# When to issue three large weight stores: one by one between the steps of the next group's blocks

## The chip, the cores and the metric

The kernel runs on one core of a Trainium2 chip. The metric is the device time of one execution in microseconds (us), lower is better. The engines are TensorE (PE; its weight loads are listed as PEld), VectorE (DVE), ScalarE (ACT), GpSimd (POOL) and SyncE (SP). SP issues every DMA of this kernel on one queue.

## The reference: two layers of linear attention and a gated MLP

The input x has 2048 rows of 512. The same two blocks run twice, with the same weights:

```
x = x + A(layernorm(x))      # linear attention, 32 heads of 16
x = x + B(layernorm(x))      # gated MLP
B(x) = (silu(x @ w1) * (x @ w3)) @ w2     # w1, w3: 512 x 1792, w2: 1792 x 512
```

All arrays are float32.

## The kernel before

**Numbers and blocks.** Every float32 factor is split into a high and a low float16 part, and a product is three float16 products (line 523). In the MLP, a further step replaces 2 x 2 block products by seven products of sums of blocks. So each weight is prepared once: raw float32 blocks are loaded, four sums and differences are formed in place, and high and low parts of the blocks and the sums are written. The inner dimension of 1792 is cut into seven groups of 256. A prepared group of w1 and w3 takes 14 KB in each partition (1792 KB), one of w2 takes 7 KB.

**Sets and passes.** On-chip memory holds four slots for groups of w1/w3. The groups are taken in sets; layer 0 has the sets (0, 1, 2), (3, 4), (5, 6). Each set runs over four passes of 512 rows, c = 0 to 3, and within a pass over its groups. `mlp_group` multiplies with w1 and w3, `first_half` and `second_half` multiply with w2. The MLP of layer 0 runs from about 195 to 600 us, the first set until about 320 us. Layer 1 reads prepared groups back from device memory, so layer 0 stores them there: groups 0 to 4 of w1/w3 are stored in the part that matters here (`w13_d`; line 757), and w2 groups 0 to 2 as well (`w2_d`, same line).

**The background.** During layer 0's MLP a generator, `background`, prepares what later sets need. After each `mlp_group`, `steps(more, budget)` takes pieces from it until their weights use up a budget from the table `HOOKS`. The generator finishes the preparation that attention has left; for groups 0, 1, 2 it prepares w2 (`w2_group`: loads at line 778, splits at lines 412 and 413) and stores it; then it takes w1/w3 group 4 and after it group 3. For group 4 it loads raw blocks (`load_raw`, line 547), stores the prepared groups 0, 1 and 2 from their slots, and makes the blocks (`w13_group`, ten yields: splits at lines 445 and 447, sums at lines 573 to 579). Group 4 is made in the fourth slot and stored from there, since group 3 will take the slot. w2 of group 4 is loaded later (line 778).

**The next rows.** While a pass runs, `mlp_rows` normalises the rows of the next one (line 500), copies them to float16 (line 1277), and transposes the high parts (line 1278) and the low parts (line 1286) by DMA; at its end it stores them (line 1290). It too is taken in pieces after each `mlp_group`.

**Order of the work.** Attention is pinned, instruction by instruction, to the order of the text. The MLP is not: a scheduler orders each engine's and the queue's instructions ahead of time. An instruction's place in the text is its rank, `later(n)` (a priority lowered by n) shifts it, and dependences hold it back. `store` is an exception:

```python
    def store(what, g, src):
        to = {"w13": w13_d, "w2": w2_d}[what]
        with in_order("SP"):
            nc.sync.dma_start(to[:, g], src)
```

`in_order("SP")` puts each such DMA behind the last DMA pinned on SP (in issue, not in completion). At run time each engine and the queue serve their instructions in the order so fixed. ScalarE copies the PSUM banks of the products out (line 1341), applies silu (line 1296), makes the hidden float16 parts (line 1300) and also does the background's splits, all in one queue.

Of the kernel before, what the change touches and what calls it, by code (L numbers as in the profile page):

```python
# [8 lines left out]
F16 = mybir.dt.float16  # L9
# [45 lines left out]
GROUP = 14 * KB  # L55
GROUP2 = 7 * KB
AT_W = 0
# [31 lines left out]
def kernel(  # L89
# [21 lines left out]
    def view(at, dtype, *dims):  # L111
        size = 4 if dtype == F32 else 2
        n = size
        for d in dims:
            n *= d
        ap = arena[:, at // 4 : (at + n) // 4]
        if dtype != F32:
            ap = ap.bitcast(dtype)
        if len(dims) > 1:
            names = "abcdefg"[: len(dims)]  # L120
            ap = ap.rearrange(
                f"p ({' '.join(names)}) -> p {' '.join(names)}",
                **{n: d for n, d in zip(names[1:], dims[1:])},
            )
        return ap
# [151 lines left out]
    @contextmanager  # L277
    def in_order(*engines):

        traced = nc.cur_bb.bb.instructions  # L280
        before = traced[-1]
        depth.append(engines)
        yield
        depth.pop()
        if depth:
            return
        start = next(k for k in reversed(range(len(traced))) if traced[k] is before) + 1
        for i in traced[start:]:
            if str(i.engine).split(".")[-1] not in (engines or PINNED):
                continue  # L290
            if i.engine in pinned:
                tc.add_manual_dep(
                    i,
                    pinned[i.engine].name,
                    mybir.DependencyInfo(
                        mybir.DependencyClass.NoSync, mybir.DependencyReason.DATA
                    ),
                    reason="in_order",
                )
            pinned[i.engine] = i  # L300
# [15 lines left out]
    def scalar():  # L316
        i = next(column)
        return scalars[:, i : i + 1]
# [28 lines left out]
    w13 = {g: view(AT_W + i * GROUP, F16, 2, 2, 2, 7, P) for g, i in SLOT13.items()}  # L347
# [74 lines left out]
    def engine_of(what, i):  # L422
        table = {what: table_of(what, state["layer"])}
        return {"V": nc.vector, "P": nc.gpsimd, "A": nc.scalar}[table[what][i]]
# [14 lines left out]
    def settle():  # L439
        while owed:  # L440
            owed.pop(0)()

    def split_late(hi, lo, src, scale):

        nc.scalar.activation(hi, src, AF.Copy, scale=scale)  # L445
        owed.append(
            lambda: nc.vector.scalar_tensor_tensor(lo, src, scale, hi, OP.mult, OP.subtract)  # L447
        )
# [91 lines left out]
    def load_raw(g):  # L540

        dst = view(AT_RAW, F32, 2, 2, 2, 2, P)
        for w, name in enumerate(("w1", "w3")):
            for c in range(2):
                for h in range(2):
                    at = h * (F // 2) + g * P
                    nc.sync.dma_start(dst[:, w, :, c, h], w_rows[name][:, c, :, at : at + P])

    def w13_group(g, dst):

        if g > 2:
            raw = view(AT_RAW, F32, 2, 2, 4, P)
            quads = [raw[:, :, :, i] for i in range(4)]
            rows = [(w, raw[:, w, :, 2:4], ((0, raw[:, w]),)) for w in range(2)]
        else:
            cols = [slice(h * (F // 2) + g * P, h * (F // 2) + g * P + P) for h in range(2)]
            quads = [st_w13[:, :, c, :, cols[h]] for c in range(2) for h in range(2)]
            both = [
                [
                    st_w13[:, w, c].rearrange("p k (h n) -> p k h n", h=2)[:, :, :, cols[0]]  # L560
                    for c in range(2)
                ]
                for w in range(2)
            ]
            rows = [(w, both[w][1], ((0, both[w][0]), (2, both[w][1]))) for w in range(2)]
        a11, a21, a12, a22 = quads
        scale = [info[n][2] for n in ("w1", "w3")]
        for w, pair, _ in rows:
            split_late(dst[:, w, 0, :, 0], dst[:, w, 1, :, 0], a11[:, w], scale[w])
            yield heavy[0]  # L570
            split_late(dst[:, w, 0, :, 1:3], dst[:, w, 1, :, 1:3], pair, scale[w])
            yield heavy[0]
        engine_of("w13", g).tensor_tensor(a22, a21, a22, OP.add)
        yield 1
        engine_of("w13", g).tensor_tensor(a21, a11, a21, OP.subtract)
        yield 1
        engine_of("w13", g).tensor_tensor(a11, a22, a11, OP.subtract)
        yield 1
        engine_of("w13", g).tensor_tensor(a12, a12, a11, OP.subtract)
        yield 1  # L580
        for w, _, parts in rows:
            for i, src in parts:
                n = src.shape[2]
                to = [dst[:, w, part, :, 3 + i : 3 + i + n] for part in range(2)]
                split_late(to[0], to[1], src, scale[w])
                yield heavy[0] * n / 2
# [167 lines left out]
# [4 lines that stand above are left out]
# [23 lines left out]
    def w2_group(g):  # L781


        raw = w2_raw(g)
        dst, scale = w2_s[g], info["w2"][2]
        yield 1
        split(dst[:, 0, 0], dst[:, 1, 0], raw[:, 0], scale)
        yield 1
        split(dst[:, 0, 1:3], dst[:, 1, 1:3], raw[:, 2:4], scale)
        yield 1  # L790
        later_plain = any(g in gs and plain_run(1, 4 * i + c) for i, gs in enumerate(SETS[1]) for c in range(NC))
        if later_plain or g in w2_a21 and state["plain"]:

            to = w2_a21.get(g, dst[:, :, 6])
            split(to[:, 0], to[:, 1], raw[:, 1], scale)
            if later_plain:
                with in_order("SP"):
                    nc.sync.dma_start(a21_d[:, g], to)
            have.add(("plain", g))
            yield 1  # L800
        a11, a21, a12, a22 = (raw[:, i] for i in range(4))
        for to, a, b, op in (
            (a22, a21, a22, OP.add),
            (a21, a11, a21, OP.subtract),
            (a11, a22, a11, OP.subtract),
            (a12, a12, a11, OP.subtract),
        ):
            engine_of("w2", g).tensor_tensor(to, a, b, op)
        yield 1
        split(dst[:, 0, 3:], dst[:, 1, 3:], raw, scale)  # L810
        yield 2
        have.add(("w2", g))

    def background(first):

        for tasks in first[::-1]:
            yield from tasks.rest()
        a, b, c = SETS[0]
        for g in a:
            yield from w2_group(g)  # L820
            store("w2", g, view(AT_W2 + SLOT2[g] * GROUP2, F16, GROUP2 // 2))
        late = view(AT_W + 3 * GROUP, F16, 2, 2, 2, 7, P)
        for g in b[::-1]:
            load_raw(g)
            if g == b[-1]:
                for i in a:
                    store("w13", i, view(AT_W + i * GROUP, F16, GROUP // 2))
            yield 1
            yield from w13_group(g, late)
            if g == b[-1]:  # L830
                store("w13", g, view(AT_W + 3 * GROUP, F16, GROUP // 2))
            settle()
            have.add(("w13", g))
            while state["plain"]:
                yield 100
            yield from w2_group(g)
        while state["set"] < 1:
            yield 100
        for g in c:
            load_raw(g)  # L840
            yield 1
            yield from w13_group(g, w13[g])
            settle()
            have.add(("w13", g))
            yield from w2_group(g)
# [309 lines left out]
    kept = []  # L1155
# [318 lines left out]

    def mlp(layer, prep):
        more = background(prep) if layer == 0 else iter(())

        def ready_for(what, g):
# [168 lines left out]
    for item in LOADS[0].split():  # L1647
        what, t = item.split(":")
        i = int(what[1:] or 0)
# [21 lines left out]
    with in_order():  # L1671
# [21 lines left out]
        b = scalar()  # L1693
# [56 lines left out]
```

## Time and profile before

| what | value |
|---|---|
| median of 3 runs | 1174.78 us (1173.83 to 1175.29) |
| profiled execution | 1172.7 us |
| its span, first to last instruction | 1170.9 us |
| mean granted TensorE clock | 0.999 |
| PE busy | 1147.1 us, 8862 matmuls |
| DVE, ACT, POOL busy | 832.0, 638.3, 402.8 us |

The profiled execution's time is 1.8 us more than its span: what lies before the first and after the last instruction. A busy share counts an engine's executing instructions; issuing DMAs and waiting don't count. Times of single rows are from the start of the span.

### The profile page before, as it was taken

Reading aid. Unit: us, or ns where it says so; the run is one execution under the profiler, and the core shown is the slowest. Engines: PE = TensorE matmul, PEld = TensorE weight load, DVE = VectorE, ACT = ScalarE, POOL = GpSimd, SP = SyncE. Lnnn points to the kernel's source line nnn. Section 1 sums busy time; section 2 is a strip of 40 time slices with the busy share of each in tenths; the row PEclk is TensorE's granted clock in tenths of the full one; section 3 lists DMA queues with packets and bytes.
Section 4 is the critical chain, followed back from the end, with each engine's and each line's share of the span. In section 5 each row is a group of like instructions: output and inputs, shape, how many; then the busy total and the mean of one; then the engine's idle time right before and its main releaser. Section 6 shows DMA issues by size and latency. Waiting matters only on the chain.

```text
span 1170.9 us, 21807 instructions
## 1 busy us (share of the span) xinstructions
PE 1147.1 (98%) x8862; PEld 863.5 (74%) x8862; DVE 832.0 (71%) x1401; ACT 638.3 (55%) x1078; POOL 402.8 (34%) x472
## 2 busy tenths in 40 slices
PE   8999998999999999999999999998999999999998
PEld 3445444788888888888864454477888888888887
DVE  6798889977977897778674568757856675656533
ACT  6677787856544554444456644766444344443422
POOL 4343588321000222113368715771252110303120
PEclk9999999999999999999999999999999999999999
DMA  9977565979632221112217425654351351111011
GB/s 279 323 235 233 122 172 119 279 257 278 155 129 100 83 81 64 64 64 73 73 41 209 122 84 116 130 144 125 86 140 64 127 189 48 50 67 37 1 37 37
DMA packets 163396, 147.43 MB, mean 126 GB/s; under 512 B 129632, under 2 KB 138976, under 8 KB 158688
## 3 DMA queue, kind: packets, MB, share of 16 engines
q1 hardware_dynamic: 163296, 146.04, 43.2%
q8 instruction: 69, 1.13, 0.4%
q14 instruction: 31, 0.25, 0.1%
HBM read 72.48 MB, written 42.07 MB: 98 GB/s over the span
## 4 chain that ended last, share of the span: by engine, by line
PE 73%; DVE 8%; DMA 6%; ACT 5%; POOL 4%; issue 2%; SPq 1%; POOLq 0%; DVEq 0%; ACTq 0%
PE bb L523 19%; PE po L1388 16%; PE bc L523 10%; PE pk L523 6%; PE gt L523 6%; PE pq L523 5%; PE po L523 5%; PE ba L523 4%; DMA arena<-arena 3%; DMA arena<-in_B_w_dram 3%; PE po L1408 2%; POOL arena L1283 1%; DVE arena L447 1%; DVE arena L1283 1%; DVE arena L1437 1%
## 5 line engine op out<-in xcount | busy, mean ns | idle before, releaser
L523 PEld LDWEIGHTS <-arena 128*128 128x128 f16 x6360 | 618.3, 98 | 251.3 <-issue 11.6
L523 PE MATMUL bb<-arena 128*128 128x256 f16 x2688 | 330.6, 273 | 4.8 <-DMA arena<-arena 2.3
L1388 PE MATMUL po<-arena 128*128 128x256 f16 x1932 | 234.8, 273 | 6.2 <-ACT arena L1300 3.2
L1388 PEld LDWEIGHTS <-arena 128*128 128x128 f16 x1932 | 188.3, 98 | 30.7 <-ACT arena L1300 5.0
L1341 ACT ACTIVATE arena<-bb 128x512 f32<-128x512 f32 x196 | 114.9, 588 | 132.7 <-PE bb L523 99.3
L523 PE MATMUL bc<-arena 128*128 128x256 f16 x1344 | 165.9, 273 | 0.3 <-DVE arena L1344 0.2
L1302 DVE TENSOR_TENSOR arena<-arena 128x512 f16<-128x512 f32 (+1 forms) x90 | 104.4, 1160 | 81.1 <-ACT arena L1300 80.9
L1300 ACT ACTIVATE arena<-arena 128x512 f16<-128x512 f32 x112 | 99.8, 891 | 104.9 <-DVE arena L1297 47.2
L1296 ACT ACTIVATE arena<-arena,scalars 128x512 f32<-128x512 f32 x112 | 74.7, 667 | 120.9 <-DVE arena L1344 119.9
L1297 DVE SCALAR_TENSOR_TENSOR arena<-arena,scalars 128x512 f32<-128x512 f32 x112 | 86.0, 768 | 50.8 <-ACT arena L1296 50.7
L1344 DVE TENSOR_TENSOR arena<-arena,bc 128x512 f32<-128x512 f32 x112 | 76.4, 682 | 57.7 <-ACT arena L1341 42.3
L1302 POOL TENSOR_TENSOR arena<-arena 128x512 f16<-128x512 f32 x22 | 25.5, 1157 | 230.9 <-ACT arena L1300 206.8
L1457 POOL TENSOR_TENSOR arena<-arena 128x512 f32<-128x512 f32 x25 | 35.7, 1428 | 195.7 <-DVE arena L1437 186.1
L1437 DVE SCALAR_TENSOR_TENSOR arena<-po,scalars,arena 128x256 f32<-128x256 f32 (+1 forms) x170 | 91.9, 584 | 6.5 <-PE po L1388 6.2
L523 PE MATMUL po<-arena 128*128 128x512 f16 x384 | 87.8, 379 | 2.1 <-DMA arena<-arena 2.0
L523 PE MATMUL ba<-arena 128*128 128x256 f16 x672 | 88.7, 274 | 0.0
L523 PE MATMUL gt<-arena 128*128 128x512 f16 x384 | 87.6, 379 | 0.6 <-ACT arena L953 0.3
L523 PE MATMUL pk<-arena 128*128 128x512 f16 x384 | 87.7, 379 | 0.0
L523 PE MATMUL pq<-arena 128*128 128x512 f16 x384 | 87.6, 379 | 0.1
L500 ACT ACTIVATE arena<-arena,nb_all,rs_all 128x512 f32<-128x512 f32 x64 | 50.2, 806 | 23.9 <-POOL nb_all L497 21.0
L1408 PE MATMUL po<-arena 128*128 128x256 f16 x480 | 57.0, 273 | 1.8 <-ACT arena L1300 1.8
L447 DVE SCALAR_TENSOR_TENSOR arena<-arena,scalars 128x512 f16<-128x512 f32 (+2 forms) x60 | 50.1, 856 | 7.9 <-ACT arena L445 6.5
(163 smaller groups left out, 1265.2 us busy)
## 6 DMA issues: line engine op xcount, KB each, us to landing
arena<-xb_d SPq DMA_DIRECT2D x12, 1792.0 KB, 6.8
xb_d<-arena SPq DMA_DIRECT2D x8, 1792.0 KB, 6.5
xt_d<-arena SPq DMA_DIRECT2D x32, 256.0 KB, 2.8
arena<-xt_d SPq DMA_DIRECT2D x32, 256.0 KB, 3.0
arena<-in_B_w_dram SPq DMA_DIRECT2D x8, 896.0 KB, 6.5
arena<-in_B_w_dram SPq DMA_DIRECT2D x28, 256.0 KB, 4.1
w_d<-arena SPq DMA_DIRECT2D x4, 1792.0 KB, 10.3
arena<-w_d SPq DMA_DIRECT2D x4, 1792.0 KB, 6.9
```

Source lines behind the costliest of these rows:

```text
L447: lambda: nc.vector.scalar_tensor_tensor(lo, src, scale, hi, OP.mult, OP.subtract)
L500: nc.scalar.activation(dst, x_sb[:, t, :], AF.Identity, scale=rs_all[:, t : t + 1], bias=nb_all[:, t : t + 1],)
L523: nc.tensor.matmul(dst, lhs(a, k), rhs(b, k), start=first and k == 0 and i == 0, stop=last and k == n - 1 and i == len(PASSES) - 1, skip_g ...
L1296: nc.scalar.activation(t, gate, AF.Silu, scale=info["u1"])
L1297: nc.vector.scalar_tensor_tensor(t, up, info["hid"], t, OP.mult, OP.mult)
L1300: nc.scalar.activation(hs[:, 0, lo:hi], t[:, lo:hi], AF.Copy)
L1302: engine.tensor_tensor(hs[:, 1, lo:hi], t[:, lo:hi], hs[:, 0, lo:hi], OP.subtract)
L1341: nc.scalar.activation(dst, bank_, AF.Copy)
L1344: nc.vector.tensor_tensor(dst, dst, bank_, OP.add)
L1388: nc.tensor.matmul(po[:, i * HALF : (i + 1) * HALF], hs[:, a, qx, cs], w2[:, b, qw, :], start=g == ends[0] and i + a + b == 0, stop=g == e ...
L1408: nc.tensor.matmul(acc[n][:, half * HALF : (half + 1) * HALF], hs[:, a, qx, cs], w2_a21[g][:, b] if (i, half) == (0, 1) else w2[:, b, i + ...
L1437: nc.vector.scalar_tensor_tensor(dst, src, cb, to, OP.mult, OP.add)
```

## The change

Before, the three stores of groups 0, 1 and 2 stand in a row in the generator, between group 4's raw load and its blocks. After, the generator's pieces for group 4 are the same with the same weights, and a store is placed in front of the yield of the fourth, the seventh and the tenth of `w13_group`'s ten steps (step numbers 3, 6, 9). Data, sizes, the store of group 4 and the pins are as before.

```diff
         for g in b[::-1]:
             load_raw(g)
             if g == b[-1]:
-                for i in a:
+                pass
+            yield 1
+            kept = list(a) if g == b[-1] else []
+            for step, weight in enumerate(w13_group(g, late)):
+                if kept and step >= (3, 6, 9)[len(a) - len(kept)]:
+                    i = kept.pop(0)
                     store("w13", i, view(AT_W + i * GROUP, F16, GROUP // 2))
-            yield 1
-            yield from w13_group(g, late)
+                yield weight
+            for i in kept:
+                store("w13", i, view(AT_W + i * GROUP, F16, GROUP // 2))
             if g == b[-1]:
                 store("w13", g, view(AT_W + 3 * GROUP, F16, GROUP // 2))
             settle()
```

In the code b is (3, 4), and the loop takes it backwards. The test `g == b[-1]` therefore holds for group 4, the first one taken.

## Rows read from the trace of the kernel before

**Rows 1.** The page's first part: busy us, share of the span, instructions of each engine.

```profile
PE 1147.1 (98%) x8862; PEld 863.5 (74%) x8862; DVE 832.0 (71%) x1401; ACT 638.3 (55%) x1078; POOL 402.8 (34%) x472
```

**Rows 2.** Windows: us, busy of each engine, granted clock, DMA share, GB/s.

```profile
235.00:240.00 5.00, 5.00 (x48) 4.47 (x47) 2.23 (x4) 2.19 (x5) 0.73 (x1) 1.00 0.31 111
...
250.00:330.00 80.00, 78.31 (x713) 69.46 (x711) 64.90 (x103) 45.36 (x74) 8.53 (x10) 1.00 0.77 229
...
250.00:272.00 22.00, 22.00 (x204) 19.71 (x202) 17.59 (x26) 12.15 (x21) 2.88 (x4) 1.00 1.08 339
...
252.50:266.70 14.20, 14.20 (x132) 12.72 (x131) 13.38 (x20) 7.87 (x13) 1.88 (x3) 1.00 1.04 402
...
309.00:313.00 4.00, 2.40 (x23) 2.00 (x22) 2.99 (x6) 2.11 (x4) 0.00 (x0) 1.00 0.51 149
...
330.00:575.00 245.00, 244.77 (x2238) 218.46 (x2236) 194.31 (x330) 113.24 (x181) 55.00 (x50) 1.00 0.25 85
...
575.00:600.00 25.00, 23.66 (x193) 18.52 (x191) 16.76 (x27) 11.19 (x16) 10.05 (x11) 1.00 0.01 1
```

**Rows 3.** Timeline of SP, 150 to 420: start us, us, line, operation, out<-in.

```profile
221.42 1.64 SPq L547 DMA_DIRECT2D arena<-in_B_w_dram  x3
...
224.31 0.88 SPq L757 DMA_DIRECT2D w_d<-arena  x1
...
246.56 1.03 SPq L757 DMA_DIRECT2D w_d<-arena  x1
247.76 3.08 SPq L547 DMA_DIRECT2D arena<-in_B_w_dram  x4
250.89 1.52 SPq L757 DMA_DIRECT2D w_d<-arena  x3
252.51 14.18 SPq L1278 DMA_TRANSPOSE arena<-arena  x1
266.78 3.05 SPq L1286 DMA_TRANSPOSE arena<-arena  x1
269.93 0.53 SPq L757 DMA_DIRECT2D w_d<-arena  x1
270.51 1.79 SPq L778 DMA_DIRECT2D arena<-in_B_w_dram  x2
```

**Rows 4.** Timeline of PE, 175 to 345; idle time before, its end, in brackets.

```profile
194.86 2.29 PE L523 MATMUL bb<-arena 128*128 128x256 f16 x10 [2.29 <-DMA arena<-arena]
...
312.10 1.47 PE L523 MATMUL bb<-arena 128*128 128x256 f16 x12 [1.60 <-ACT arena L1341]
```

**Rows 5.** Timeline of ACT, 215 to 345, with the same brackets.

```profile
236.81 1.52 ACT L412 ACTIVATE arena<-arena,scalars 128x256 f16<-128x256 f32 x3 [2.37 <-DMA arena<-in_B_w_dram]
...
248.86 1.04 ACT L1277 ACTIVATE arena<-arena 128x1024 f16<-128x1024 f32 x1
...
271.10 1.88 ACT L1277 ACTIVATE arena<-arena 128x512 f16<-128x512 f32 x3 [0.82 <-DMA arena<-arena]
...
277.97 1.37 ACT L412 ACTIVATE arena<-arena,scalars 128x256 f16<-128x256 f32 x2 [0.39 <-DMA arena<-in_B_w_dram]
...
309.81 1.76 ACT L412 ACTIVATE arena<-arena,scalars 128x256 f16<-128x256 f32 x3 [1.63 <-DMA arena<-in_B_w_dram]
```

**Rows 6.** The chain that ended last, 195 to 345: start us, us, what.

```profile
270.99 7.61 DMA arena<-in_B_w_dram
...
302.41 2.48 DVE arena L447 x2
...
306.67 4.16 DMA arena<-in_B_w_dram
```

**Rows 7.** Timeline of DVE, 245 to 270.

```profile
264.51 2.48 DVE L447 SCALAR_TENSOR_TENSOR arena<-arena,scalars 128x1024 f16<-128x1024 f32 x2 [0.36 <-ACT arena L445]
```

**Rows 8.** Windows of 2 us behind the wait at 194.86.

```profile
195.00:197.00 2.00, 2.00 (x11) 1.37 (x10) 1.97 (x6) 0.98 (x2) 2.00 (x2) 0.50 0.26 50
197.00:199.00 2.00, 2.00 (x15) 1.56 (x14) 1.06 (x3) 1.97 (x6) 2.00 (x3) 0.71 0.43 123
```

## The prediction

> **What bounds the kernel now.** I began with the page's busy shares [rows 1]: TensorE is busy for 1147.1 of 1170.9 us. All it can ever give back is 23.8 us, and only where a change makes one of its waits shorter. So I went to the stretches around the first set of layer 0's MLP [rows 2]. From 250 to 272 us, when the three stores are moved, PE is busy for 22.00 of 22.00 us. From 250 to 330 it is busy for 78.31 of 80.00: it loses 1.69 us, and 1.60 of them between 309 and 313, where it is busy for 2.40 of 4.00. From 330 to 575 it loses 0.23 of 245 us. What is near the stores can therefore return 1.7 us at most, 0.14% of the time.
>
> Third I read the order on SP's queue [rows 3]. The three stores (line 757) are issued at 250.89, 1.52 us for all three. Right behind them stands the first of two transposes of the next rows (line 1278), which holds the queue for 14.18 us, until 266.7, while the stores drain; the second (line 1286) follows at 266.78. The fourth store is issued at 269.93, the loads for group 4's w2 blocks at 270.51. This is what looks wrong in the profile, and the reader is to see that PE does not feel it: the 22 us of [rows 2] cover the hold from end to end.
>
> Last I asked which wait does reach PE [rows 4, 5]. ScalarE's queue is served in order. At 309.81 splits of w2 (line 412), 1.76 us of them, follow 1.63 us of waiting for a load; the copy of a PSUM bank (line 1341) comes behind them, and PE starts at 312.10 after 1.60 us idle for that copy. The load that belongs to the stores' neighbourhood is that of 270.51: it took 7.61 us to land [rows 6], and ScalarE's split of it waited 0.39 us, at 277.97. So a load that lands later there meets a queue with hardly any slack.
>
> **The change part by part.** *Removed and added:* no instruction, no byte. Seven stores of this kind run before and after, three of them elsewhere in the program's text. Issue is 1.52 us on SP for three, the same for one by one, and SP does no arithmetic. Zero.
>
> *Moved in the text.* The generator gives the same steps with the same weights, so the hooks' budgets take the same pieces; only the stores fall later, past step 3, 6 and 9 of group 4's ten. But the order in the text isn't the order of issue: outside the pinned part the scheduler takes what is ready, and the text only ranks what is ready together. The rows show it. Group 4's raw load is written after all three w2 stores of groups 0 to 2, yet its first half is issued from 221.42 on, before the first of them, at 224.31; its other half, whose buffer was still in use, at 247.76 [rows 3]. The three stores are held by one thing, the pin of `store` behind the last pinned store on SP, at 246.56. Their data is done: the first pass has multiplied with groups 0 to 2. After the change they hang on the same pin, on no step of group 4. So they are ready at the same moment as before, and the next thing on SP that could overtake them is the first transpose, whose last input, a copy on ScalarE of 1.04 us at 248.86 [rows 5], ends at 249.90. Either the three are still issued in a row, and nothing has changed, or one or both transposes get in front of some of them.
>
> *If the transposes get in front.* The 14.18 us of hold go, or shrink to what is left of a store or two. One store's transfer is 1792 KB, 1.835 MB, at the 402 GB/s of the stretch from 252.5 to 266.7 [rows 2]: 4.6 us, so behind one store the transpose is held some 5 us. What does an earlier landing give? ScalarE's next row copies waited 0.82 us for these transposes, to 271.10 [rows 5], and PE waited for nothing then. Bounds: from nothing (PE had no idle time there) to the 0.09 us that PE lost in this stretch outside 309 to 313, plus, if the whole background chain up to the w2 load before 309.81 moves forward with it, the 1.60 us. I take nothing: that load (306.67) follows the last splits of group 3's blocks (line 447, 302.41) in the chain of waits [rows 6], and those wait for no transpose of these rows.
>
> *What is late instead.* Every store that goes behind a transpose drains later, and the queue serves the fourth store and the w2 loads behind it. Before, the three were gone by 266.7, so only the fourth store lay ahead of the loads. In the worst order the third store goes only as step 9 is done (its last splits on VectorE, line 447, end at 264.51 + 2.48 = 266.99 [rows 7]); then its 4.6 us stand in front, the loads land near 283.2 instead of 270.99 + 7.61 = 278.6 [rows 6], and the split waits 0.39 + 4.6 = 5.0 us. What PE pays is bounded by two rows of ScalarE: the wait of 2.37 us before 236.81 cost PE nothing (from 235 to 240 it is busy for 5.00 of 5.00 us [rows 2]); the wait of 1.63 us before 309.81 cost 1.60 [rows 4, 5]. So between nothing and 5.0 us; I take the middle of 5.0 - 2.4 = 2.6, with the cover of the first row, and 5.0, with that of the second: 3.8. This is the price of a rival, not of the forecast, since nothing makes the stores wait for the steps.
>
> *The ranks of others.* The lines between the old and new places move up by three in the text. What runs under a lowered priority there may swap with a neighbour, and the scheduler may then order engines a little differently further on. The nearest rows for what that can move: the 1.69 us lost near the stores and the 1.34 us lost from 575 to 600 [rows 2], where layer 0 ends. Either sign; I take nothing.
>
> *The skill.* The Trainium skill, page "DMA: Bandwidth & Descriptors", section "Queues, rings and completion order", says that each DMA engine consumes a queue's descriptors in ring order. By this rule, spreading the stores saves no transfer time and only chooses what stands behind them; the loads at 270.51 could only get later. The trace agrees: the loads of 256 KB behind the fourth store took 7.61 us [rows 6].
>
> The sum: 0 us. The profiled execution took 1172.7 us, its span of 1170.9 and 1.8 around it, and is 2.1 us below the median of the three runs, 1174.78. The forecast stands on the median: 1174.8. A difference of 0.2%, 2.3 us, is about the least that can be told from no change here, since the three runs lie within 1.5 us.
>
> **The rivals.**
>
> *The queue doesn't change.* The stores stay in a row, as above; the time is the forecast's. I put it inside the forecast, as its likelier half.
>
> *Slower: late loads hold ScalarE.* The third store (or two) drains in front of the w2 loads. It decides from about 2.4 us of extra lateness on. For it: the slack of 0.39 us, and DMA already at 1.08 of 16 engines' time from 250 to 272 [rows 2]. Against it: the stores are ready by 247 and SP is free to issue them. 1174.8 + 3.8 = 1178.6 us. A gap of that length may cost the clock too: PE stood 2.29 us before 194.86, and the granted clock was 0.50 and 0.71 in the next two stretches of 2 us [rows 4, 8], the first of them at the lower of the two levels, 1.2 GHz; that took (0.50 + 0.29) x 2 = 1.6 us, and would make 1180.2. The Trainium skill, page "TensorE: Matmul & The Clock Gate", section "Part 1: The HAM clock gate", says the same, that an idle TensorE falls back to half rate until it has been busy again.
>
> *Faster: the losses near and after the stores vanish.* The chain of rows and w2 blocks runs ahead, ScalarE no longer stands before 309.81, and the end of the layer falls better. All of 1.69 + 1.34 = 3.0 us: 1171.8. For it: the hold of 14.18 us is real and is released. Against it: two places 260 us apart would both have to gain, and either alone stays under 2.3 us.
>
> **How the numbers follow.** The forecast, no change that can be told, has 0.62 (0.37 the same queue, 0.25 transposes in front at no gain to PE); late loads 0.20; losses gone 0.18. Each rival lies beyond 0.2%, so these are also the chances of same, slower and faster. The forecast's own range is 1172.5 to 1177.1. The range for 8 in 10 reaches to the faster case, 1171.8, and nearly to the slower one, 1178.5; beyond them I leave half of the slower case and a little of the faster, under 2 in 10.
>
> **What would show it.** On SP: whether three issues of line 757 still stand in one row before the transpose of line 1278, and whether that one still takes about 14 us. On ScalarE: the wait before the first line 412 of group 4, 0.39 us before; over 2.4 us means the slower rival. On PE: 22.00 of 22.00 us where the stores drain, and 1.60 us at 312. What would make me wrong: PE idle time in a place that has nothing to do with the stores, in the second set or in layer 1, from a schedule that has come out otherwise; no row of before prices that.

## The result, and the profile after

The changed kernel is slower: 1179.91 us median (1179.52 to 1180.88, six runs) against 1175.58 us (1173.83 to 1177.66, six runs) on the same chip. The ratio is 1.0043, 95% interval [1.0032, 1.0053]. That is above the upper end of the predicted range, 1178.5 us.

The profile after is one execution of 1179.52 us, span 1177.6 us. Its line numbers behind the edit are those of before plus 6 (L1278 is L1284, L1341 is L1347, L1388 is L1394). The first part of the page answers to [rows 1]:

```profile
PE 1147.1 (97%) x8862; PEld 863.4 (73%) x8862; DVE 832.7 (71%) x1401; ACT 638.8 (54%) x1078; POOL 402.8 (34%) x472
```

TensorE does the same work in the same 1147.1 us; the span grew by 6.7 us, all of it idle time. The windows of [rows 2] again, in the kernel after:

```profile
250.00:330.00 80.00, 75.96 (x689) 66.99 (x687) 61.24 (x98) 43.13 (x70) 7.24 (x9) 1.00 0.70 217
250.00:272.00 22.00, 20.84 (x192) 18.52 (x190) 18.43 (x28) 13.96 (x23) 6.08 (x8) 1.00 1.06 337
...
309.00:313.00 4.00, 4.00 (x39) 3.60 (x37) 4.00 (x7) 0.72 (x1) 0.00 (x0) 1.00 0.01 4
330.00:575.00 245.00, 242.10 (x2206) 215.31 (x2205) 194.70 (x329) 112.62 (x179) 54.53 (x51) 1.00 0.26 89
575.00:600.00 25.00, 24.27 (x212) 20.46 (x210) 15.90 (x27) 9.66 (x15) 9.79 (x11) 1.00 0.00 1
```

The reader is to see two things. The old gap is gone (309 to 313: 4.00 of 4.00, before 2.40). But 250 to 330 lost 4.04 us instead of 1.69, and 330 to 575 lost 2.90 instead of 0.23. The granted clock stays at 1.00. The first matmul of layer 1 that both traces show behind the same small gap (gt, L523) starts at 613.96 us before and at 619.91 after, 5.95 us later; the other 0.75 us of the 6.7 fall behind it, where every engine's order is the same in both kernels.

What became of SP's queue ([rows 3] before):

```profile
246.51 1.03 SPq L757 DMA_DIRECT2D w_d<-arena  x1
247.71 3.08 SPq L547 DMA_DIRECT2D arena<-in_B_w_dram  x4
250.83 0.47 SPq L757 DMA_DIRECT2D w_d<-arena  x1
251.40 6.41 SPq L1284 DMA_TRANSPOSE arena<-arena  x1
257.90 3.30 SPq L1292 DMA_TRANSPOSE arena<-arena  x1
261.26 1.06 SPq L757 DMA_DIRECT2D w_d<-arena  x2
263.52 0.32 SPq L1296 DMA_DIRECT2D xb_d<-arena  x1
267.55 3.07 SPq L547 DMA_DIRECT2D arena<-in_B_w_dram  x3
270.66 1.57 SPq L757 DMA_DIRECT2D w_d<-arena  x1
272.28 3.85 SPq L778 DMA_DIRECT2D arena<-in_B_w_dram  x2
```

One store, then both transposes, then two stores. The hold shrank from 14.18 to 6.41 us. But more moved than the stores: the store of the transposed rows (L1296, 272.50 us before) and three of group 3's raw loads now go ahead of the fourth store, and the loads of w2 go behind them. (The fourth store is group 4's. The page counts four stores of 1792 KB, those of groups 0, 1, 2 and 4; group 3's prepared weights are not stored.)

TensorE from 250 to 450 us, every line with idle time ahead of it ([rows 4] before, where 312.10 was the only one in this stretch):

```profile
265.03 1.47 PE L523 MATMUL bb<-arena 128*128 128x256 f16 x12 [1.16 <-ACT arena L1347]
...
302.11 1.47 PE L523 MATMUL bb<-arena 128*128 128x256 f16 x12 [1.11 <-ACT arena L1347]
...
322.19 1.47 PE L523 MATMUL bb<-arena 128*128 128x256 f16 x12 [0.99 <-ACT arena L1347]
...
325.23 1.59 PE L1394 MATMUL po<-arena 128*128 128x256 f16 x13 [0.70 <-ACT arena L1306]
...
330.69 1.47 PE L523 MATMUL bc<-arena 128*128 128x256 f16 x12 [0.60 <-DVE arena L1303]
...
367.91 1.59 PE L1394 MATMUL po<-arena 128*128 128x256 f16 x13 [0.49 <-ACT arena L1306]
...
374.26 0.39 PE L1394 MATMUL po<-arena 128*128 128x256 f16 x2 [0.17 <-ACT arena L1306]
...
381.07 1.59 PE L1394 MATMUL po<-arena 128*128 128x256 f16 x13 [0.93 <-ACT arena L1306]
...
431.76 0.49 PE L1394 MATMUL po<-arena 128*128 128x256 f16 x3 [0.30 <-DVE arena L1443]
...
432.48 0.39 PE L1394 MATMUL po<-arena 128*128 128x256 f16 x2 [0.24 <-ACT arena L1306]
```

Ten small waits, 6.69 us together, in place of one of 1.60. None is for a DMA. Each is for a copy out of PSUM (L1347), a finished hidden part (L1306) or a step of VectorE on the same data (L1303, L1443). ScalarE's timeline shows what stood in front of them ([rows 5] before):

```profile
262.10 1.89 ACT L1283 ACTIVATE arena<-arena 128x512 f16<-128x512 f32 x3 [1.62 <-DMA arena<-arena]
263.89 0.61 ACT L1306 ACTIVATE arena<-arena 128x512 f16<-128x512 f32 x1
264.41 0.57 ACT L1347 ACTIVATE arena<-bb 128x512 f32<-128x512 f32 x1
...
284.55 0.51 ACT L412 ACTIVATE arena<-arena,scalars 128x256 f16<-128x256 f32 x1 [0.17 <-DMA arena<-in_B_w_dram]
...
299.00 0.51 ACT L445 ACTIVATE arena<-arena,scalars 128x256 f16<-128x256 f32 x1 [4.57 <-DMA arena<-in_B_w_dram]
299.42 0.71 ACT L1302 ACTIVATE arena<-arena,scalars 128x512 f32<-128x512 f32 x1
300.94 0.63 ACT L1306 ACTIVATE arena<-arena 128x512 f16<-128x512 f32 x1 [0.82 <-DVE arena L1303]
301.48 0.58 ACT L1347 ACTIVATE arena<-bb 128x512 f32<-128x512 f32 x1
...
320.75 0.91 ACT L412 ACTIVATE arena<-arena,scalars 128x256 f16<-128x256 f32 x2 [2.88 <-DMA arena<-in_B_w_dram]
321.56 0.57 ACT L1347 ACTIVATE arena<-bb 128x512 f32<-128x512 f32 x1
```

Row copies (L1283) wait 1.62 us for the transposes ahead of the L1347 for which TensorE waits at 265.03; a split (L445) waits 4.57 us for a load, and the L1347 of 302.11 comes three places behind it; splits of w2 (L412) wait 2.88 us ahead of the L1347 of 322.19. The place that the slower rival named is quiet: the first L412 of group 4 waits 0.17 us, at 284.55. The Trainium skill, page "PSUM — Partial Sum Buffer", section "Engine vs sequencer instructions", says that ScalarE's and VectorE's queues are strictly first in, first out, and that matmuls start in program order; the trace agrees: at 299.00 everything behind the waiting split waited with it.

So the scheduler had made its order anew. Comparing the two built programs, 993 of TensorE's 8845 instructions stand elsewhere, all among its numbers 1495 to 2903, 156 of VectorE's 1369, 92 of ScalarE's 1026 and 28 of SP's 326; none of GpSimd's, and none behind some 435 us.

### The profile page after: what moved, and what is told of

Read it like the earlier page. It is cut to its first block, busy times and chain, and to the rows that moved or that the text cites. A ratio compares the mean times of both kernels' runs of the same rounds, so it can differ in the third digit from the quotient of the medians.

```text
span 1177.6 us, 21810 instructions
## 1 busy us (share of the span) xinstructions
PE 1147.1 (97%) x8862; PEld 863.4 (73%) x8862; DVE 832.7 (71%) x1401; ACT 638.8 (54%) x1078; POOL 402.8 (34%) x472
## 4 chain that ended last, share of the span: by engine, by line
PE 67%; DVE 12%; DMA 7%; ACT 6%; POOL 5%; issue 3%; SPq 1%; DVEq 0%; POOLq 0%; ACTq 0%
PE bb L523 17%; PE po L1394 14%; PE bc L523 9%; PE pk L523 6%; PE gt L523 5%; PE pq L523 5%; PE po L523 5%; DMA arena<-arena 4%; PE ba L523 4%; DMA arena<-in_B_w_dram 3%; PE po L1414 2%; DVE arena L1443 1%; POOL arena L1289 1%; DVE arena L1350 1%; DVE arena L413 1%
## 5 line engine op out<-in xcount | busy, mean ns | idle before, releaser
L523 PEld LDWEIGHTS <-arena 128*128 128x128 f16 x6360 | 618.7, 98 | 254.6 <-issue 14.7
L523 PE MATMUL bb<-arena 128*128 128x256 f16 x2688 | 329.8, 273 | 7.1 <-ACT arena L1347 4.5
L1394 PE MATMUL po<-arena 128*128 128x256 f16 x1932 | 234.4, 273 | 8.6 <-ACT arena L1306 5.3
L1394 PEld LDWEIGHTS <-arena 128*128 128x128 f16 x1932 | 187.9, 98 | 34.5 <-ACT arena L1306 8.4
L1347 ACT ACTIVATE arena<-bb 128x512 f32<-128x512 f32 x196 | 115.0, 589 | 134.1 <-PE bb L523 104.6
L523 PE MATMUL bc<-arena 128*128 128x256 f16 x1344 | 165.9, 273 | 1.2 <-DVE arena L1303 0.6
L1306 ACT ACTIVATE arena<-arena 128x512 f16<-128x512 f32 x112 | 99.8, 891 | 103.2 <-DVE arena L1321 44.3
L1303 DVE SCALAR_TENSOR_TENSOR arena<-arena,scalars 128x512 f32<-128x512 f32 x112 | 86.0, 767 | 51.8 <-ACT arena L1302 51.6
L1443 DVE SCALAR_TENSOR_TENSOR arena<-po,scalars,arena 128x256 f32<-128x256 f32 (+1 forms) x170 | 91.8, 582 | 6.2 <-PE po L1394 5.9
L523 PE MATMUL po<-arena 128*128 128x512 f16 x384 | 87.8, 379 | 2.0 <-DMA arena<-arena 2.0
L523 PE MATMUL ba<-arena 128*128 128x256 f16 x672 | 89.5, 275 | 0.0
L523 PE MATMUL gt<-arena 128*128 128x512 f16 x384 | 87.6, 379 | 0.6 <-ACT arena L959 0.3
L523 PE MATMUL pk<-arena 128*128 128x512 f16 x384 | 87.6, 379 | 0.5 <-DMA arena<-arena 0.3
L523 PE MATMUL pq<-arena 128*128 128x512 f16 x384 | 87.6, 379 | 0.1
L500 ACT ACTIVATE arena<-arena,nb_all,rs_all 128x512 f32<-128x512 f32 x64 | 50.1, 806 | 24.1 <-POOL nb_all L497 21.1
```

Source lines behind the costliest of these rows:

```text
L500: nc.scalar.activation(dst, x_sb[:, t, :], AF.Identity, scale=rs_all[:, t : t + 1], bias=nb_all[:, t : t + 1],)
L523: nc.tensor.matmul(dst, lhs(a, k), rhs(b, k), start=first and k == 0 and i == 0, stop=last and k == n - 1 and i == len(PASSES) - 1, skip_g ...
L1303: nc.vector.scalar_tensor_tensor(t, up, info["hid"], t, OP.mult, OP.mult)
L1306: nc.scalar.activation(hs[:, 0, lo:hi], t[:, lo:hi], AF.Copy)
L1347: nc.scalar.activation(dst, bank_, AF.Copy)
L1394: nc.tensor.matmul(po[:, i * HALF : (i + 1) * HALF], hs[:, a, qx, cs], w2[:, b, qw, :], start=g == ends[0] and i + a + b == 0, stop=g == e ...
```

## The experiments

Most kernels are the kernel before with its text untouched and a table that chains each engine's instructions of this stretch in a given order (no instruction is added, no semaphore either):

```python
for item in table.split():
    at, n = (int(v) for v in (item + "+1").split("+")[:2])
    for i in by[engine][at : at + n]:
        if before is not None:
            tc.add_manual_dep(i, before.name, ...)   # NoSync
        before = i
```

Numbers in the tables are an engine's instructions in the text's order. On SP, 154 to 156 are the three stores, 157 and 158 the two transposes, 160 the fourth store, 162 and 163 the w2 loads of group 4, 159 the store of the transposed rows.

For all of them, this is what TensorE lost from 250 to 450 us in the profiled execution (200 less its busy time there), beside the ratio of the times. The row for the kernel before, from its windows:

```profile
250.00:450.00 200.00, 198.09 (x1804) 175.91 (x1802) 164.76 (x269) 104.62 (x167) 31.30 (x31) 1.00 0.46 147
```

| kernel | lost, us | ratio to before [95%] |
|---|---|---|
| before | 1.91 | 1 |
| after | 6.94 | 1.0043 [1.0032, 1.0053] |
| e1 queue only | 3.03 | 1.0000 [0.9991, 1.0009] |
| e2 copies back | 8.40 | 1.0041 [1.0026, 1.0056] |
| e3 w2 loads first | 6.42 | 1.0026 [1.0014, 1.0037] |
| e4 both back | 5.68 | 1.0030 [1.0018, 1.0041] |
| e5 first part after | 5.27 | 1.0017 [1.0007, 1.0027] |
| e6 second part after | 5.27 | 1.0026 [1.0016, 1.0036] |
| e7 two stores late | 7.64 | 1.0051 [1.0036, 1.0065] |
| e8 after, held | 5.73 | 1.0048 [1.0034, 1.0063] |
| e9 splits behind | 7.41 | 1.0057 [1.0043, 1.0070] |
| e10 one copy ahead | 2.27 | 1.0005 [0.9997, 1.0014] |
| e11 matmul order only | 14.52 | 1.0121 [1.0102, 1.0140] |
| e12 all but matmuls | 16.16 | 1.0134 [1.0114, 1.0154] |
| e13 steps 1, 2, 3 | 3.99 | 1.0002 [0.9990, 1.0013] |
| e14 steps 2, 4, 6 | 8.50 | 1.0053 [1.0037, 1.0069] |
| e15 steps 9, 10, 11 | 11.44 | 1.0084 [1.0067, 1.0101] |
| e16 w2 rows swapped | 6.67 | 1.0048 [1.0033, 1.0063] |

What is lost in this stretch goes with the time, roughly: after minus before is 5.03 us, and 0.0043 of 1175.58 is 5.06. That the two meet so closely is luck, since each row is one execution. Built, e13 is the program of before, instruction by instruction, and its row is 3.99, not 1.91; e8 is the program of after, and its row is 5.73, not 6.94.

The column counts idle time alone. In before, after and e8 the granted clock stayed at 1.00 in this stretch. Behind one gap each in e4, e7, e14 and e15, and behind two in e11, it fell to the lower level, 1.2 GHz: in e7 it was 0.80 from 312 to 316 us and 0.78 from 316 to 320. That is (0.20 + 0.22) x 4 = 1.7 us more, which the column leaves out.

I had two readings to tell apart at first: the order made anew, or the moved transfers themselves.

**e1: the stores moved, nothing else.** Every engine's order is that of before; in the queue alone, the transposes overtake two stores.

```diff
 "SP": 154
-155 156 157 158
+157 158 155 156
 160 162+2 159
```

> The kernel before with one thing moved on SP's queue: the two transposes of the next rows stand behind the first of the three stores and in front of the other two, as in the kernel after. All engines and the rest of the queue are held in the order of before. Theory A (the loss comes from the other instructions that the scheduler has put in another order): the time of before within 0.2%, 1173.5 to 1178 us; the first transpose is held about 6 us instead of 14, and PE loses no more than before from 250 to 330 us, 1.7 us. Theory B (the loss comes from stores that now drain in front of the fourth store and the loads of w2): the loads land up to 4.6 us later, ScalarE's split of them waits up to 5 us instead of 0.39, and the time is 1178 to 1180 us.

1175.38 us, ratio 1.0000. Its queue:

```profile
251.15 0.50 SPq L757 DMA_DIRECT2D w_d<-arena  x1
251.75 7.00 SPq L1278 DMA_TRANSPOSE arena<-arena  x1
258.85 2.81 SPq L1286 DMA_TRANSPOSE arena<-arena  x1
261.71 5.88 SPq L757 DMA_DIRECT2D w_d<-arena  x3
267.63 2.58 SPq L778 DMA_DIRECT2D arena<-in_B_w_dram  x2
```

The hold is 7.00 us instead of 14.18, and nothing is gained or lost. The moved stores are out as the cause; the loads that moved with them are put back in e3.

**e8: the control.** The whole order of after, held by the table over the text of before.

```diff
-"PE", "DVE", "Activation", "SP": order of before
+"PE", "DVE", "Activation", "SP": order of after
```

> Control: the kernel before with every engine and the queue held in the order of the kernel after; the same order as after, instruction by instruction. All theories: the time of after, 1179 to 1181 us; anything else would mean that holding an order costs or saves time by itself.

1180.43 us, ratio 1.0048. The program so built is that of after, instruction by instruction, and its time is that of after: the tables reproduce an order and add nothing of their own.

**e2, e3, e4: which part of the order?** All three hold the order of after, with the row copies (by the lines of before, ScalarE's L1277 and L500, VectorE's L1283) put back where before had them; with the fourth store and group 4's w2 loads put back ahead of the row store; and with both.

```diff
 e2  "Activation": 351 352 353 365 366, "DVE": 459 460 461
+     each behind its neighbour in the order of before
 e3  "SP":
+160 162 163
 159
```

> The kernel after, in its own order, with one thing put back: on ScalarE the three float16 copies of the last rows and two normalisations, and on VectorE the three subtractions behind the copies, stand where they stood before. Theory A1 (the copies that were put in front of the work for PSUM wait for transposes that are not done, and hold ScalarE): the 1.16 us that PE is idle before 265.0 go, with the same loss afterwards; 1178.3 to 1179 us, 0.1% less than after. Theory A2 (the loss is the chain of loads and blocks behind it): the gaps from 302 us on stay and make up at least 3 us of the 5 to 6. If the copies set everything: the time of before.

> The kernel after, in its own order, but on SP's queue the fourth store and group 4's two w2 loads stand in front of the store of the rows and of group 3's raw loads, as before. Theory A2 (the loads of w2 that were put behind these free the second half of the staging buffer late, so group 3's blocks and w2 come late and ScalarE stands waiting for them): group 3's second raw half lands by 293 instead of 299 us, the waits of 4.57 and 2.88 us on ScalarE shrink, the gaps at 302, 322 and 330 us shrink with them, and the time is 1176 to 1177.5 us. Theory A1 (only the copies): no change from after, 1179.5 us.

> Both of the last two together: the copies where they were, and the fourth store and the w2 loads in front. The stores still stand one before and two behind the two transposes. If the two mechanisms make up the loss: 1175 to 1176.5 us, the time of before within 0.2%. If it comes from the order of the matmuls or of ScalarE's and VectorE's other instructions further on, which stays as in after: 1178 us or more.

e2: 1180.37 us. The gap at 265 went, one of 0.63 came at 292.00, and that of 374.26 grew from 0.17 to 1.78 us (at 376.36). The copies aren't the loss. e3: 1177.91 us, but not by what was expected: layer 0 ends where it did (gt at 619.76, after 619.91), with gaps of 1.01, 1.07 and 0.93 us at 265.10, 302.14 and 380.57, where after has 1.16, 1.11 and 0.93. Its 2 us came in layer 1, whose orders are the same (555.74 us from gt to the end, after 557.69). Most of them lie in one wait of TensorE for VectorE (L1437, in after L1443): 0.38 us at 830.44, in after 1.66 us at 832.49. The same wait is 0.42 us in e7, which is no faster than after. I can't say why; one profile of each can't settle it. e4: 1178.16 us, with fewer but larger gaps (2.11 us at 302.88). No single suspect carries it.

**e5, e6: which half?** At some 320 us all engines' orders hold the same instructions behind them, so each can be cut there and joined. By a drain the expectations mean the tail of the last matmul before a gap, which the profile counts as busy: 12 matmuls alone take 1.47 us, 24 in one piece 2.78 (before, 215.25), so a gap adds some 0.16.

```diff
 "PE" 1943, "DVE" 484, "Activation" 382, "SP" 180
+e5: order of after up to these, then that of before
+e6: order of before up to these, then that of after
```

> All engines and the queue have the order of the kernel after up to about 320 us, where the first set ends, and the order of before from there on; the cut lies where both orders have issued the same instructions. Theory F (the first set: w2 and group 3's blocks come late, and whatever stands behind them pays): 1178.5 to 1180 us, with gaps again between 320 and 440 us. Theory S (the second set: the order of ScalarE and TensorE from 320 to 440 us leaves the gaps at 325, 331, 368, 381 and 433 us that were the same in four traces): the gaps up to 302 us stay, 1.16 + 1.11 us less the 1.60 of before, and the time is 1176 to 1177 us.

> The other half: the order of before, with the three stores in a row, up to about 320 us, and the order of after from there on. No store is issued where it was moved to. Theory S: the gaps from 325 to 433 us are there, some 3 us with 0.2 us of drain each, and the time is 1178.5 to 1180 us. Theory F: the time of before within 0.2%.

1177.23 and 1177.83 us, ratios 1.0017 and 1.0026. Neither theory came as priced: both halves lose, and within their intervals they add up to the whole, 0.43%. In e6 the three stores stand in a row as before, and it loses no less than e5.

**e7: two stores much later.** Groups 1 and 2 are stored after group 3's w2 blocks; the order is left to the scheduler.

```diff
-                for i in a:
-                    store("w13", i, view(AT_W + i * GROUP, F16, GROUP // 2))
+                store("w13", a[0], view(AT_W + a[0] * GROUP, F16, GROUP // 2))
...
+            if g == b[0]:
+                for i in a[1:]:
+                    store("w13", i, view(AT_W + i * GROUP, F16, GROUP // 2))
```

> The kernel before, but the stores of groups 1 and 2 stand in the text behind group 3's w2 blocks, where the profile of before has little traffic (from 313 to 330 us DMA is busy for 0.21); group 0's stays. Nothing is held, so the scheduler makes an order of its own: on SP group 3's first raw loads come in front of the fourth store and the w2 loads, as in after, and the transposes stand behind one store. If traffic in front of the loads made the loss: the time of before or up to 1.7 us less. If the order does: a loss like that of after, 1178 to 1181 us, though 3584 KB have left the place.

1180.51 us, ratio 1.0051, with gaps of 1.08, 1.46 and 2.88 us at 265.97, 294.90 and 313.92: another order, other gaps, the same size of loss. Behind the last of them the clock fell as told under the table, so that some 1.7 us of this execution are the clock's.

**e9, e10: who stands in front?** My theory by now: splits that wait for a load stand in front of copies. e9 is the order of after with those steps put behind; e10 is the order of before with its one such place mended.

```diff
 e9  "Activation"            "DVE"
-    351+3 ... 306           478 ... 415
+    306 351+3               415 478
-    380 ... 341             512 514 ... 513 437
+    341 380                 437 512 514 513
-    394 396 358
+    358 394 396
-    446+2 391 399, 488 403 406
+    391 399 446+2, 403 406 488
 e10 "Activation"
-    394 396 395 343
+    343 394 396 395
```

> The order of the changed kernel on all engines, but on ScalarE and VectorE the steps that waited for a load stand behind the copies of PSUM that they held up: ScalarE's copies of the last rows behind the next L1341, one L445 split of 256 columns behind the L1341 that followed it, two L412 splits behind the next L1341, the two L445 splits of 1024 columns and one of 512 behind the next L1341; VectorE's L447 and L413 of the same blocks behind the L1297 and the L1315 after them. Theory (in the re-made order, splits that wait for a load or for VectorE hold up the copies that empty PSUM): the gaps of TensorE at about 265, 302, 322, 325, 368 and 374 us (1.16, 1.11, 0.99, 0.70, 0.49 and 0.17 us, 4.62 us together, and some 0.17 us of drain for each, 1.0 us) go, those of 330.7 (0.60), 381 (0.93) and 432 us (0.54) stay, and the time falls by 4 to 5.6 us: ratio to the kernel before 0.9995 to 1.001. Rival (the new order of the matmuls itself runs out of finished hidden parts, whoever stands in front of whom): the gaps come back some microseconds later, the sum of them up to 450 us stays above 5 us, and the ratio is 1.003 or more.

> The kernel before in its own order on every engine but for one step: ScalarE's copy L1341 that ran at 311.48 us stands ahead of the three L412 splits of 309.81 us, which wait 1.63 us for their load, not behind them. Theory (such a place is what costs the changed kernel its time): the gap of 1.60 us of TensorE at 312.10 us goes with its drain of some 0.17 us, nothing comes later in its place, ratio to the kernel before 0.9983 to 0.9988, some 1173.5 us. Rival (a gap closed there is taken up by the next wait, since the loads are no sooner): the gap moves to between 313 and 335 us with at least half its size, ratio 0.9993 to 1.0005.

Both fell to the rival. e9: 1179.89 us, ratio 1.0057, nothing won. Its TensorE:

```profile
305.39 1.47 PE L523 MATMUL bb<-arena 128*128 128x256 f16 x12 [0.52 <-ACT arena L1341]
...
328.48 1.47 PE L523 MATMUL bc<-arena 128*128 128x256 f16 x12 [1.47 <-DVE arena L1297]
...
369.40 0.83 PE L1388 MATMUL po<-arena 128*128 128x256 f16 x6 [1.46 <-DVE arena L1302]
```

and ScalarE ahead of the first of them:

```profile
304.13 0.72 ACT L445 ACTIVATE arena<-arena,scalars 128x512 f16<-128x512 f32 x1 [2.83 <-DMA arena<-in_B_w_dram]
304.76 0.58 ACT L1341 ACTIVATE arena<-bb 128x512 f32<-128x512 f32 x1
```

The next split of the chain now does what the mended one did. e10: 1174.27 us, ratio 1.0005; the 1.60 us at 312.10 are gone, and 0.81 stand at 313.85. Its other gaps, 0.36 at 275.11, 0.54 at 378.29 and 0.16 at 427.74, can't be put down to the edit. The program of before, executed again in e13, has gaps at the first two places without it:

```profile
275.23 1.47 PE L523 MATMUL bb<-arena 128*128 128x256 f16 x12 [0.48 <-DVE arena L1350]
...
313.48 1.47 PE L523 MATMUL bb<-arena 128*128 128x256 f16 x12 [2.01 <-ACT arena L1347]
...
379.86 1.47 PE L523 MATMUL bb<-arena 128*128 128x256 f16 x12 [1.19 <-ACT arena L1347]
```

So the mended gap did shrink, but the times show no gain: the theory asked for 0.9983 to 0.9988. A waiting step ahead of a copy is how a gap looks, not what the loss hangs on.

**e11, e12: one engine's order against the others'.** e11 takes TensorE's order of after and all else of before; e12 the reverse.

```diff
-e11 "PE": order of before
+e11 "PE": order of after
-e12 "DVE", "Activation", "SP": order of before
+e12 "DVE", "Activation", "SP": order of after
```

> TensorE issues its matmuls in the order of the changed kernel (993 of its 8845 stand elsewhere), while ScalarE, VectorE, GpSimd and the queue of SyncE keep the order of the kernel before, three stores in a row included. Theory P (the matmul order is what is dear: it asks for a finished hidden part or a free buffer of PSUM some hundred ns too soon): gaps of TensorE between 250 and 435 us of 5 us and more together, ratio to the kernel before 1.003 to 1.006. Theory Q (the order on the other engines and of the loads is what is dear): gaps there of under 3 us, as before, ratio 0.9990 to 1.0012. Theory M (each order fits only its own partner): as P in this run, or worse.

> The other half: TensorE keeps the matmul order of the kernel before, while ScalarE, VectorE and the queue of SyncE have that of the changed kernel, with the store, two transposes, two stores, the loads of the second set's group 3 ahead of the fourth store. Theory P: gaps of TensorE between 250 and 435 us of under 3 us together, ratio 0.9990 to 1.0012. Theory Q: 5 us and more, above all where ScalarE's copies wait behind splits (near 265, 302 and 322 us), ratio 1.003 to 1.006. Theory M: as Q in this run, or worse, so that both mixes are slower than the kernel before.

1189.43 and 1190.78 us, ratios 1.0121 and 1.0134: each mix loses some three times what the whole order of after loses. From e12's TensorE:

```profile
346.59 1.47 PE L523 MATMUL bb<-arena 128*128 128x256 f16 x12 [3.20 <-ACT arena L1341]
...
364.50 1.48 PE L523 MATMUL bc<-arena 128*128 128x256 f16 x12 [1.69 <-DVE arena L1297]
```

Theory M held. The loss sits neither in the matmul order of after alone nor in the orders of the others alone: each is dearer with the partner from before than the two are together.

**e13 to e16: is it the stores at all?** Three other placings between the steps, and an edit that touches no store. The order is left to the scheduler.

```diff
-                if kept and step >= (3, 6, 9)[len(a) - len(kept)]:
+                if kept and step >= (1, 2, 3)[len(a) - len(kept)]:    e13
+                if kept and step >= (2, 4, 6)[len(a) - len(kept)]:    e14
+                if kept and step >= (9, 10, 11)[len(a) - len(kept)]:  e15
...
-        for i, f in enumerate((g, NG + g)):                            e16
+        for i, f in ((1, NG + g), (0, g)):
```

> The changed kernel, but its three stores stand behind steps 1, 2 and 3 of group 4's blocks, not 3, 6 and 9; the order is made anew. Theory L (the change costs by the order that happens to be made anew, not by the place of the stores): gaps of TensorE in other places between 250 and 435 us with another sum, so a ratio that is its own, anywhere from 0.998 to 1.007. Theory F (stores between the steps are themselves dear, since they let transposes and loads in between): 1.003 to 1.006, as with the changed kernel, with gaps in the same places (265, 302, 322, 325 us).

> As the run before, with the stores behind steps 2, 4 and 6; its order stands nearer to that of the changed kernel than the other two. Theory L: near the changed kernel where the orders agree, else a ratio of its own between 0.998 and 1.007. Theory F: 1.003 to 1.006.

> As before, with the stores behind steps 9, 10 and 11, which lets both transposes and more of the loads in front of the stores. Theory L: a ratio of its own between 0.998 and 1.007. Theory F: 1.003 to 1.006 or, as more of the transfers come ahead of the stores, above that.

> The kernel before with its stores in a row; only the two loads of each w2 group stand in the other sequence in the text (the second half of the rows first). The same bytes move, no store is touched, and the order is made anew on all engines between 190 and 435 us. Theory L: a ratio of its own, off 1.000 by over 0.002 to either side, with gaps of TensorE in new places. Theory F: 0.999 to 1.001, gaps as in the kernel before.

e13: 1175.09 us, ratio 1.0002. Its stores stand between steps in the text, but not in the program. Built, it is the kernel before, instruction by instruction on every engine and on the queue, with the same waits; so it moved nothing, and is a second measurement of the kernel before. Its queue shows the old row of three and the old hold:

```profile
251.14 1.56 SPq L757 DMA_DIRECT2D w_d<-arena  x3
252.80 14.43 SPq L1284 DMA_TRANSPOSE arena<-arena  x1
```

e14, 1.0053, and e15, 1.0084, were made anew, each with gaps of its own (2.12 us at 382.63 in e14; 1.85 at 261.95 and 2.11 at 386.72 in e15). In e15 the last two stores stand behind the last of the ten steps, and its ratio lies above the range that theory L gave it. And e16, which touches no store and keeps the row of three with its hold, loses as much as the change:

```profile
252.01 1.86 SPq L757 DMA_DIRECT2D w_d<-arena  x3
253.92 14.03 SPq L1278 DMA_TRANSPOSE arena<-arena  x1
```

1180.86 us, ratio 1.0048, with these among its gaps from 250 us on:

```profile
281.04 1.70 PE L1408 MATMUL po<-arena 128*128 128x256 f16 x14 [1.29 <-ACT arena L1300]
...
309.53 0.39 PE L1388 MATMUL po<-arena 128*128 128x256 f16 x2 [2.65 <-ACT arena L1300]
```

Not all of e16's loss lies in this stretch, since its order changes from some 200 us on: at 222.45 TensorE waits 2.59 us (before 1.57 at 220.91), the granted clock is 0.50 from 224 to 226 us, and from 190 to 250 us TensorE gets through 433 matmuls instead of 457, some 2.6 us' worth. From 250 to 450 us it loses 6.67 us, the program of before 1.91 and 3.99.

Stores moved in the queue and every engine's order kept (e1): nothing. Order made anew, in part or whole, and the three stores in a row (e6, e16): 0.26 and 0.48%. That settles what the loss belongs to, the order made anew and not the moved stores. Which part of the order it is, no run shows.

## Why the prediction was wrong

*What bounds the kernel*: right. TensorE is the bound, the hold of SP was covered, and releasing it gave nothing (e1). "What is near the stores can therefore return 1.7 us at most" is right too, as a bound on a gain: the gap of 1.60 us did go. It bounds no loss, and I let it stand for both signs.

*Removed and added: zero*: right, by e1.

*Moved in the text*: right on the stores. Of its two cases the second came, and e13 is the first, at 1.0002. But the two cases leave out that other transfers may change places as well: the row store and three raw loads went ahead of the fourth store.

*If the transposes get in front*: right. The hold fell to 6.41 us, where I had some 5, and PE gained nothing by it.

*What is late instead*, the slower rival: the loads of group 4's w2 were issued 1.77 us later (272.28), but the split that I named waited 0.17 us, not over 2.4, since it had been moved as well (284.55 instead of 277.97). The 1.6 us of clock that I put on top didn't come either: the granted clock stayed at 1.00 behind all ten waits. That rival's time, 1178.6, came near what was measured by another mechanism than its own, which is luck.

*The ranks of others: "either sign; I take nothing"*: this step failed. I priced it at the idle time of the nearest rows, 1.69 and 1.34 us, and set it to nothing. In fact the scheduler made 185 us of the program anew on four engines, and TensorE lost 6.94 us there (5.73 in e8, the same program) where the program of before lost 1.91 (3.99 in e13). The rows of before can't price this: they show one order, and its idle time says nothing about the next one's. I had said so in the last part ("no row of before prices that") and still gave it no chance of its own. What the runs showed in its place: five orders that the scheduler made anew (after, e7, e14, e15, e16) cost 0.43, 0.51, 0.53, 0.84 and 0.48%, about 5 to 10 us; where every engine's order stayed (e1), nothing.

Open: why all five are slower and none faster. That the kernel before has an uncommonly good order would explain it, but these samples don't show it. They are fewer than five, too: after, e7, e14 and e15 were built with one and the same order on every engine from some 380 us on, e14 and e15 from some 335. Open is also the difference in layer 1 between e3 and the kernel after.

## What to carry to other kernels

Before an edit is priced, compare the built order of each engine with the old one: if it is unchanged, as in e13, nothing was changed; if only the moved instructions differ, the price is theirs; if it is made anew over a stretch in which TensorE is 99% busy, the idle time in the old profile bounds only the gain, and here the loss was 0.4 to 0.8%. Move such a thing inside a held order, as e1 does, and it shows its own worth, here nothing. Mending the gaps of a given order one by one won nothing here (e9, e10), and exchanging one engine's order alone cost three times the whole loss (e11, e12): the orders of TensorE, ScalarE, VectorE and the queue fit as a set.

## What the runs showed of the hardware

A DMA transpose issued behind 1792-KB stores holds SP's queue longer by about the same for each: 3.06 us with none of the three in front (e15, 252.02), 6.41 with one (after; 7.00 in e1), 10.43 with two (e14, 252.42), 14.18 with three [rows 3] (14.03 in e16, 14.43 in e13).

```profile
252.42 10.43 SPq L1284 DMA_TRANSPOSE arena<-arena  x1
```

```profile
252.02 3.06 SPq L1284 DMA_TRANSPOSE arena<-arena  x1
```

By the first figure of each that is 3.4 to 4.0 us for a store, less than the 4.6 us that I had estimated from the stretch's rate.

Two executions of the same program needn't show the same gaps: before lost 1.91 us of TensorE's time from 250 to 450 us, and e13, the same program, 3.99, with 0.48 us at 275.23 and 1.19 at 379.86 where the other has none. A single small gap is thus no evidence, and the sum over a stretch is off by some 2 us; the repeated times are what counts.

How long TensorE stands doesn't settle alone whether the clock falls. It fell behind 2.12 us (e14, 382.63; 0.63 from 384 to 388) and behind 2.29 (before, 194.86; 0.50 from 195 to 197). It stayed at 1.00 behind 2.29 us in e7 (195.35), whose order up to there is that of before, and behind 3.20 us in e12 (346.59).
